# Norm factor of batch 6 taken through DRAM like batch 7's, in a replanned order (linear attention, RMS norm and gated convolution FFN on one core)

## Chip, core and metric

The kernel runs on one core of one Trainium2 chip. The metric is the device time of one execution in microseconds (us). The program is fully unrolled: each engine (PE for matmuls, DVE, ACT, POOL, and SP, which here only issues DMAs) has its own queue of instructions that it works off in order, and semaphores tie the queues together.

## The reference

For each of 8 batches and 8 heads, with 576 rows and head size 64:

```python
kv  = einsum('bhsd,bhse->bhde', k, v)            # 64 x 64 per head
out = einsum('bhsd,bhde->bhse', q, kv)
x   = out / sqrt(mean(out*out, -1) + 1e-6) * g_norm      # per head and row
x   = x.transpose(0, 2, 1, 3).reshape(B, S, 512)
h    = relu(x @ w_in)                                    # 512 -> 1024
conv = sum over 3 rows of conv_w * h (zero padded)       # per channel
y    = (h * sigmoid(conv)) @ w_out                       # 1024 -> 512, float32
```

## The kernel before, in words

Channels lie on partitions, rows on the free axis. Heads go in pairs (four tiles `t` of 128 channels), the 1024 hidden channels in eight tiles `f`, and batches in pairs `p` for the FFN. `ORDER` is a string of tokens that is written out by hand or by a planner; a loop calls one small function per token, in that order, and the order in the string is also the order on every engine's queue. A token reads `name.arguments@slots:choice`: the slots are PSUM banks or the numbers of ring buffers, and the choice says whether ACT or DVE makes a copy or a relu. So a wait of one token holds up all later tokens on the same engine.

The tokens that matter here:

- `Lq`, `Lk`, `Lv` (L301), `Li` and `Lo` load q, k, v of a batch, quarters of `w_in` and halves of `w_out`. POOL issues them. A full batch needs three loads of 576 KB in bf16.
- `kv` (L358) makes the 64 x 64 states on PE. For batches 0 to 3, `qt`/`qc` transpose q on PE, `ot` multiplies. For batches 5, 6 and 7, `dq` (L436) transposes q by two DMAs from SP, `kvn` copies the state out of PSUM, `kx` (L449) copies it with halves swapped by two small DMAs from SP, and `oq` (L464) multiplies in 64 x 64 array tiles.
- `sq` and `oc` (L493, L341, on ACT) square and copy the product out of PSUM.
- The norm factor: `ss` (L575) sums the squares on PE for a group of batches (`NORM`: batch 6 is group 3, batch 7 group 4), `ln` (L584) takes the reciprocal root on ACT. After that there are two ways to spread the factor over the 64 channels of a head. **By PE:** `sl` (L591 to L594) splits it on DVE into bf16 parts, `sp` (L603) multiplies these with a 0/1 matrix, eight products for a batch, and `mu` (L629) multiplies x with the factor in PSUM. **Through DRAM** (batches in `FD`): `fw` (L610) writes the root to DRAM, `fr` (L617) reads it back broadcast to 64 partitions, two DMAs for each half of the rows, and `mu` (L625) multiplies with the factor in SBUF. Both DMAs are issued by SP.
- `hm` (L640) is the first FFN product, eight matmuls for one `f` of one batch, `re` (L646, L648) its relu, `ta`, `aa`, `ab`, `sg`, `mg` the convolution, sigmoid and gate on DVE and ACT (`cm`, L714, makes some of it on PE), `om` and `oh` (L744, L759) the second product, `ea` and `eh` its copy out of PSUM, `st` and `sh` (L778, L773) the stores, issued by SP.
- `unread` (L427) runs matmuls whose result nobody reads.

Of the kernel before, what the change touches and what calls it, by code (L numbers as in the profile page):

```python
# [67 lines left out]
pre@0,0,0 unread.10@0 qt0.0.0@0 ps pn qc0.0.0:1@0 pi ca.k.0 ca.v.0 kv.0.0.1@1 kvc.0.0.1.0:1@0 kvc.0.0.1.1 al.h0@0
ct@2 pg qt0.0.1@3 Lq.1.0@1 qc0.0.1:1 ot.0.0@0 Li.1 pc dg.6:1 sq.0.0@0 Li.3 unread.3@4 kv.0.1.1@3 kvc.0.1.1.0:1
dg.7:1 kvc.0.1.1.1:1 al.h1@1 Lv.1.0@1 al.x0@0 on.0.0@4 nl.0.0@0 mu0.0.0 Lk.1.0@1 Li.0 al.x1@1 unread.1@6 qt0.0.2@2  # L70
ot.0.1@6 sq.0.1@1 Lq.1.2 unread.3@3 kv.0.2.1@3 kvc.0.2.1.0:1 on.0.1@4 qt0.0.3@0 kvc.0.2.1.1:1 qc0.0.2:1@1 nl.0.1@1
mu0.0.1 ot.0.2@2 unread.3@1 kv.0.3.1@1,4 Lv.1.2 sq.0.2@2 qc0.0.3:1 kvc.0.3.1.0:1 kvc.0.3.1.1 on.0.2@6 ot.0.3@4
nl.0.2@2 mu0.0.2 sqh.0.3.0@3 unread.3@0 onh.0.3.0@6 sqh.0.3.1 nlh.0.3.0@3 onh.0.3.1 qt.1.0@2 nlh.0.3.1 qc.1.0:1@2
muh.0.3.0 muh.0.3.1 hm.0.2@6 re.0.2 hm.0.3@4 hm.0.6@6 re.0.3 ta.0.2@0 pl re.0.6 Lk.1.2 ta.0.3 aa.0.1 hm.0.7@4
re.0.7:1 cm.0.6@6 kv.1.0.2@2 kvc.1.0.2.0:1@1 sg.0.6@1 Lq.2.0@0 cm.0.7@4 kvc.1.0.2.1 Lv.2.0@0 ot.1.0@2 sg.0.7
hm.0.1@6 sq.1.0@4 qt.1.1@4 ab.0.1 on.1.0@0 nl.1.0@4 Lk.2.0@0 re.0.1:1 hm.0.0@6 re.0.0 qc.1.1@3 mg.0.3 mu0.1.0
ot.1.1@4 sq.1.1@5 kv.1.2.2@0 ta.0.0@1 kvc.1.2.2.0 kvc.1.2.2.1 on.1.1@2 nl.1.1@5 Li.2 ta.0.1 ot.1.2@0 Lq.3.0@1
ot.1.3@6 Lv.3.0@1 Lk.3.0@1 sq.1.2@6 aa.0.0 sq.1.3@7 mu0.1.1 ab.0.0 unread.1@2 on.1.2@2 nl.1.2@6 on.1.3@4 nl.1.3@7
sg.0.1 sg.0.0 qt.2.1@2 qt.2.0@4 mu0.1.2 mu0.1.3 hm.1.2@0 hm.1.3@6 re.1.2 qc.2.0@4 qc.2.1@0 mg.0.0 ta.1.2@1 hm.1.1@2
hm.1.6@0 re.1.3 kv.2.0.4@6 ta.1.3 aa.1.1 hm.0.5@4 ab.1.1 sg.0.2 re.1.1 sg.0.3 re.1.6 kvc.2.0.4.0@0 sg.1.3  # L80
kvc.2.0.4.1:1 mg.0.1 Lo.0 hm.0.4@0 ot.2.2@6 re.0.5 Lo.1 re.0.4:1 sg.1.2 mg.1.1 ta.0.4@0 ot.2.0@4 sq.2.2@0 sq.2.0@1
ta.0.5 hm.1.7@2 hm.1.4@0 re.1.7 oc.2.2@0 aa.0.2 hm.1.5@2 ot.2.1@6 re.1.4 ta.1.4@1 ab.0.2 oc.2.0@1 Lq.4.0@0 re.1.5
sq.2.1@2 qt.3.1@0 oc.2.1 sg.0.4 sg.0.5 qt.3.0@4 hm.1.0@2 ot.2.3@6 ta.1.5 qc.3.1@1 Lq.5.0@1 unread.3@0 kv.3.0.4@0
qc.3.0@2 aa.1.2 mg.0.2 sq.2.3@3 ss.2@1 kvc.3.0.4.0:1@1 kvc.3.0.4.1:1 oc.2.3 re.1.0 ln.8@0 unread.3@4 ot.3.1@2
ot.3.2@6 ot.3.0@4 ta.1.0@0 ta.1.1 ab.1.2 sq.3.2@4 oc.3.2@2 om.0.0.0@0 om.0.1.0@1 om.0.3.0@6 sq.3.0@5 oc.3.0@3
ot.3.3@4 aa.1.0 sl.8@0 om.0.1.4 sq.3.1@6 ab.1.0 om.0.3.4 oc.3.1 Lk.4.0@0 sq.3.3@7 oc.3.3 sp.2.1@2,4 ea.0.1@0
Lv.4.0@0 ea.0.3@1 mu.2.1.0 dq.5.0@3 ss.3@7 Lv.5.0@1 ln.1@0 om.0.0.4 mu.2.1.1 sp.2.0@6,2 om.0.2.0@1 qtp.4.1@4
mu.2.0.0 sg.1.5 ea.0.0@2 mu.2.0.1 hm.2.7@6 sg.1.4 om.0.2.4 qc.4.1@4 re.2.7 ea.0.2@3 sg.1.0 sg.1.1 sl.1@0 hm.2.2@4
sp.3.0@0,6 mg.1.2 mu.3.0.1 hm.2.5@2 mu.3.0.0 mg.1.0 re.2.2 cm.1.6@6 re.2.5 cm.1.7@0 dq.5.1@0 sg.1.6@1 hm.2.4@2
sg.1.7 sp.3.1@0,6 kv.4.0.4@4 mg.1.3 re.2.4 kvn.4.0.4 qtp.4.0@2 mu.3.1.0 Lk.5.0@1 ky.4.0.4.0 ky.4.0.4.1 mu.3.1.1  # L90
qc.4.0@2 hm.3.4@0 al.x2@0 hm.3.5@6 oq.4.0@2 re.3.4 re.3.5 ta.2.4@0 oq.4.1@0 hm.2.6@4 ta.2.5 sq.4.0@0 oc.4.0@1
hm.3.3@6 hm.3.6@2 re.2.6 sq.4.1@1 re.3.3 Lk.7.0@0 oc.4.1 Lv.7.0@0 hm.3.7@4 hm.3.1@0 re.3.6 aa.2.2 re.3.7 ab.2.2
om.0.6.0@4 hm.3.2@2 sg.2.5 re.3.1 sg.2.4 ta.2.6@1 ta.2.7 Lq.7.0@0 om.0.6.4 oq.4.3@0 oq.4.2@6 kv.5.0.4@5 re.3.2
aa.2.3 ea.0.6@4 Lk.6.0@1 ab.2.3 hm.2.3@2 Lv.6.0@1 sq.4.2@2 om.0.4.0@4 kvn.5.0.4:1 ky.5.0.4.0:1 ky.5.0.4.1:1 sq.4.3@3
oc.4.2@0 oq.5.0@6 oc.4.3 re.2.3 oq.5.1@0 sq.5.0@4 mg.2.2 sq.5.1@5 om.0.8.0@5 om.0.4.4 oc.5.0@3 st.0.0 ss.4@2 oc.5.1
oq.5.3@6 ea.0.4@5 oq.5.2@0 ta.2.2@0 sq.5.3@6 sq.5.2@7 om.0.8.4 ta.2.3 om.0.5.0@4 ss.5 om.0.5.4 ln.2@0 hm.2.0@2
# [5 lines left out]
hm.5.0@0 sg.2.0 sg.2.1 ta.3.2@1 re.5.0 Lq.6.0@1 ta.3.3 hm.5.5@6 hm.4.7@2 aa.3.1 re.4.7 hm.4.0@4 re.4.0 hm.4.1@0
hm.5.6@4 re.5.5 ab.3.1 mg.2.0 re.4.1 dq.7.1@2 st.0.4 kx.6.0.4.0 hm.5.4@6 om.1.5.0@0 ta.3.0@0 sg.3.2 sg.3.3 st.0.6
st.0.3 re.5.4 oq.7.3@2 re.5.6 oq.7.2@6 sq.7.3@2 kx.6.0.4.1 om.1.8.0@1 dq.6.0@4 dq.6.1@3 ta.3.1 st.0.5 sq.7.2@3
st.0.2 st.0.1 ea.1.5@5 oc.7.2@0 ss.7@4 om.1.4.0@0 hm.5.7@6 ln.4@0 oc.7.3 oq.6.0@2 oq.6.2@4 ea.1.4@4 ea.1.8@1 mg.3.1
# [6 lines left out]
re.6.0 st.1.5 st.1.2 hm.6.1@6 re.6.3 re.7.4 re.6.1 st.1.6 aa.4.3 hm.7.1@2 mg.3.3 re.7.1 ab.4.3 sg.4.7 hm.6.4@4
hm.7.5@2 st.1.1 hm.7.0@6 hm.6.5@0 sg.4.6 re.6.4 re.7.0 st.1.3 re.7.5 om.2.4.0@4 re.6.5 om.2.7.0@5 om.2.1.0@0
ta.4.2@0 ta.4.3 om.2.2.0@1 aa.4.1 ea.2.4@5 mg.4.3 ab.4.1 om.2.0.0@4 ta.4.0@1 ta.4.1 sg.4.2 om.2.5.0@2 sg.4.3 aa.4.0
mg.4.1 ab.4.0 ta.4.4@0 ea.2.7@3 ea.2.1@4 ea.2.2@6 ta.4.5 st.2.4 sg.4.1 sg.4.0 st.1.0 st.2.7 st.2.2 aa.4.2 ab.4.2
ea.2.0@0 om.2.3.0@3 ea.2.5@5 om.2.6.0@2 om.2.8.0@4 sg.4.5 mg.4.0 st.0.8 st.2.5 om.3.4.0@5 sg.4.4 mg.4.2 ea.2.6@2
ea.2.3@3 om.3.7.0@3 om.3.4.4 ea.2.8@6 st.2.1 om.3.7.4 om.3.0.0@4 om.3.3.0@2 om.3.0.4 om.3.6.0@1 om.3.5.0@0 om.3.6.4
st.2.6 st.1.8 st.2.8 ea.3.4@7 ea.3.7@5 om.3.5.4 st.2.0 st.3.4 om.3.1.0@3 st.2.3 om.3.3.4 om.3.1.4 om.3.2.0@5
ea.3.0@4 ea.3.6@2 oh.3.8.0@6 ea.3.5@1 ea.3.3@6 om.3.2.4 oh.3.8.1 ea.3.1@0 st.3.5 st.3.7 st.3.6 st.3.0 eh.3.8.0@7
ea.3.2@3 st.3.3 st.3.1 sh.3.8.0 eh.3.8.1 st.3.2 sh.3.8.1  # L120
"""


# [705 lines left out]
```

## Time and profile before

| | |
|---|---|
| median of 3 runs | 179.23 us (179.04 to 180.67) |
| the profiled execution | 179.07 us, span 177.3 us, granted clock 1.0 |
| PE busy | 170.7 us (96% of the span), 1663 matmuls |
| ACT busy | 150.4 us (85%), 233 instructions |
| DVE busy | 138.4 us (78%), 235 instructions |
| POOL busy | 30.6 us (17%), 54 instructions |
| DMA queues | software 59.2%, SP's 27.4% of 16 engines' span |
| `dq`, from issue to landing: shortest, median, longest | 3.7, 10.9, 15.8 us |

The span is the time from the first to the last profiled instruction; 1.8 us of the execution lie around it. A busy PE is not a PE at its peak, since matmuls overlap in the array; what counts for PE is the time from the start of one product to the start of the next. A time such as 36.73 us is counted from the start of the span.

### The profile page before, as it was taken

The page shows a single profiled execution, that of the slowest core. Times are in us where ns is not written, and L with a number is a line of the kernel's source. Part 1 is how long each engine was busy: PE and PEld are TensorE (multiplying, and loading weights), DVE is VectorE, ACT ScalarE, POOL GpSimd, SP SyncE. Part 2 cuts the span into 40 slices and gives each one's busy share as a digit, 9 for nine tenths or more (in the row PEclk, how much of TensorE's full clock was granted, in tenths as well). Part 3 has the DMA queues.
Part 4 walks back from the last instruction along what each step waited for, and adds up shares of the span by engine and source line. Part 5 has one row for each costly group of instructions (what it writes and reads, how often), then busy time and mean ns, then how long its engine had stood idle before and what let it go on. Part 6 is the DMA issues. An engine that isn't in the chain of part 4 may idle for free.

```text
span 177.3 us, 4089 instructions
## 1 busy us (share of the span) xinstructions
PE 170.7 (96%) x1663; PEld 101.8 (57%) x1663; DVE 138.4 (78%) x235; ACT 150.4 (85%) x233; POOL 30.6 (17%) x54
## 2 busy tenths in 40 slices
...
GB/s 144 198 199 199 200 204 204 203 204 206 205 204 203 197 191 141 190 204 204 189 165 123 117 203 132 33 180 292 153 118 0 4 0 178 122 153 307 14 276 199
DMA packets 36219, 29.49 MB, mean 166 GB/s; under 512 B 8528, under 2 KB 31720, under 8 KB 36200
## 3 DMA queue, kind: packets, MB, share of 16 engines
q0 software_dynamic: 21760, 15.96, 59.2%
q1 hardware_dynamic: 14400, 13.26, 27.4%
q8 instruction: 13, 0.21, 0.5%
q14 instruction: 6, 0.05, 0.1%
...
## 4 chain that ended last, share of the span: by engine, by line
PE 76%; DMA 14%; POOL 5%; ACT 2%; issue 1%; POOLq 0%; ACTq 0%
PE bank L744 33%; PE bank L640 30%; DMA w_in_sb<-in_moe_w_in_dram 9%; DMA k_sb<-in_k_dram 5%; PE bank L358 2%; PE bank L464 2%; POOL q_sb L241 1%; PE bank L603 1%; PE bank L575 1%; POOL k_sb L241 1%; POOL v_sb L241 1%; PE bank L759 1%; PE bank L431 1%; PE bank L714 1%; POOL w_in_sb L315 1%
## 5 line engine op out<-in xcount | busy, mean ns | idle before, releaser
L640 PE MATMUL bank<-xT,w_in_sb 128*128 128x288 bf16 x512 | 66.4, 286 | 0.1
L744 PE MATMUL bank<-w_out_sb,h 128*128 128x512 bf16 x280 | 64.5, 379 | 0.0
L640 PEld LDWEIGHTS <-w_in_sb 128*128 128x128 bf16 x512 | 49.1, 98 | 14.7 <-issue 0.6
L744 PEld LDWEIGHTS <-h 128*128 128x128 bf16 x280 | 26.3, 98 | 30.7 <-issue 2.1
L646 ACT ACTIVATE h<-bank 128x576 bf16<-128x576 f32 x61 | 37.9, 657 | 3.1 <-PE bank L640 2.6
L728 ACT ACTIVATE taps<-taps,cwn 128x1152 bf16<-128x1152 bf16 (+1 forms) x36 | 38.0, 1093 | 1.4 <-DVE taps L695 1.3
L341 ACT ACTIVATE row<-bank 128x512 f32<-128x512 f32 (+1 forms) x37 | 21.0, 589 | 11.7 <-PE bank L744 10.0
L734 DVE TENSOR_TENSOR h<-h,taps 128x2304 bf16<-128x2304 bf16 (+1 forms) x20 | 22.3, 1114 | 3.0 <-ACT taps L728 1.8
L689 DVE TENSOR_TENSOR taps<-taps 128x2304 bf16<-128x2304 bf16 (+1 forms) x18 | 20.9, 1160 | 0.4
L695 DVE TENSOR_TENSOR taps<-taps,h 128x2304 bf16<-128x2304 bf16 (+1 forms) x18 | 20.8, 1153 | 0.2
L682 DVE TENSOR_SCALAR taps<-h,cwn 128x1152 bf16<-128x1152 bf16 (+1 forms) x36 | 17.4, 483 | 2.5 <-ACT h L646 2.4
L493 ACT ACTIVATE sq<-bank 128x576 bf16<-128x576 f32 x28 | 17.9, 674 | 0.0
L629 DVE SCALAR_TENSOR_TENSOR xT<-o,cw,bank 128x576 bf16<-128x576 f32 x20 | 15.4, 810 | 2.1 <-PE bank L603 1.9
L683 DVE TENSOR_SCALAR taps<-h,cwn 128x1152 bf16<-128x1152 bf16 (+1 forms) x36 | 16.9, 469 | 0.0
L341 ACT ACTIVATE o<-bank 128x576 f32<-128x576 f32 x24 | 16.0, 682 | 0.0
...
L427 PE MATMUL bank<-fill 128*128 128x512 bf16 x30 | 10.1, 462 | 1.6 <-DVE fill L228 1.5
L301 POOL DMA_DIRECT2D k_sb<-in_k_dram x8 | 6.0, 750 | 26.5 <-PE bank L358 25.7
L301 POOL DMA_DIRECT2D q_sb<-in_q_dram x8 | 6.1, 760 | 17.4 <-PE bank L380 15.1
L358 PEld LDWEIGHTS <-k_sb 96*64 96x64 bf16 x384 | 7.2, 114 | 3.0 <-issue 2.4
L358 PE MATMUL bank<-v_sb,k_sb 96*64 96x64 bf16 x384 | 8.5, 199 | 0.0
L562 DVE SCALAR_TENSOR_TENSOR xT<-bank,cw,root 128x576 bf16<-128x576 f32 x7 | 5.6, 814 | 1.8 <-ACT root L542 1.7
...
## 6 DMA issues: line engine op xcount, KB each, us to landing
...
```

Source lines behind the costliest of these rows:

```text
L341: nc.scalar.activation(to, fr, AX.Copy)
L358: nc.tensor.matmul(ps[i][i * D:(i + 1) * D, t - t0, :], k_sb[:, 2 * t + i, r * D:(r + 1) * D], v_sb[:, 2 * t + i, r * D:(r + 1) * D], star ...
L493: nc.scalar.activation(in_order(b, s), product(b, t), AX.Square)
L640: nc.tensor.matmul(ps[:, e, :HS], w_in_sb[:, t, f * P:(f + 1) * P], x[:, t, e * HS:(e + 1) * HS], start=(t == 0), stop=(t == NT - 1))
L646: nc.scalar.activation(to, fr, AX.Relu)
L682: nc.vector.tensor_scalar_mul(tap[:, 0, f % 2, :n, 8:8 + S], h[:, f], cwn[:, 0, f:f + 1])
L683: nc.vector.tensor_scalar_mul(tap[:, 1, f % 2, :n, :S], h[:, f], cwn[:, 2, f:f + 1])
L689: nc.vector.tensor_add(tap[:, 1, :, :n, :S], tap[:, 0, :, :n, 7:7 + S], tap[:, 1, :, :n, 1:1 + S])
L695: nc.vector.tensor_add(y, y, h[:, 2 * j:2 * j + 2])
L728: nc.scalar.activation(y, y, AX.Sigmoid, scale=cwn[:, 1, f:f + 1])
L734: nc.vector.tensor_mul(h, h, T["tap", c, j][:, 1, :, :n, :S])
L744: nc.tensor.matmul(T["om", p, m], h[:, f, m * P:(m + 1) * P], w_out_sb[:, f, :], start=(f == 0), stop=(f == NF - 1))
```

## The change

`FD` becomes `(6, 7)`. Batch 6's factor now goes the way that batch 7's goes: `fw.3`, and `fr.6.0`, `fr.6.1` (four DMAs) are added to SP's queue, into the rings of the k tiles that are free by then. `sl.3` (four DVE instructions) and `sp.6.0`, `sp.6.1` (eight products) are gone, and batch 6's four `mu` read SBUF instead of PSUM. One of 30 `unread` matmuls is gone. Thirteen copies and relus change between ACT and DVE. Everything else is the same set of tokens in a new order, with new banks. Cut to what is spoken of below:

```diff
-FD = (7,)
+FD = (6, 7)
 ...
 ORDER = """
...
-oc.5.2@2 oc.5.3 ea.0.5@6 re.2.0 dq.7.0@1 hm.2.1@0 aa.2.1 ea.0.8@7 ab.2.1 re.2.1 sl.2@0 sp.4.1@6,2 mu.4.1.1 mu.4.1.0
-om.0.7.0@4 sp.4.0@0,2 kv.7.0.4@5 mu.4.0.0 om.0.7.4 mu.4.0.1 sg.2.3 sp.5.0@0,6 sg.2.2 kvn.7.0.4:1 ea.0.7@2 mu.5.0.1
...
-sq.6.0@4 fw.4 fr.7.0@0 st.1.4 aa.3.0 re.5.7 oc.6.0@3 ta.3.4@1 sq.6.2@5 om.1.6.0@0 oc.6.2@2 oq.6.3@6 oq.6.1@2
-om.1.7.0@1 sq.6.1@6 ta.3.5 ab.3.0 sq.6.3@7 aa.3.2 ab.3.2 ss.6@4 oc.6.3 ln.3@0 sl.3@0 oc.6.1 ea.1.7@6 om.1.0.0@5
-om.1.2.0@1 mu.7.0.1 mu.7.0.0 sg.3.0 sg.3.1 sp.6.0@2,6 mu.6.0.0 mu.6.0.1 fr.7.1@1 mg.3.0 om.1.3.0@4 st.0.7 st.1.7
-ea.1.2@3 hm.4.6@6 ea.1.3@0 om.1.1.0@4 ea.1.6@4 re.4.6 ea.1.0@2 mu.7.1.0 sp.6.1@6,0 mu.7.1.1 ta.3.6@0 mu.6.1.1 sg.3.5
-ta.3.7 al.h3@1 hm.7.3@2 mu.6.1.0 ea.1.1@6 hm.7.7@4 hm.7.6@0 sg.3.4 aa.3.3 hm.6.2@6 re.7.3 re.7.7 hm.6.6@4 re.7.6
...
+om.0.8.4 sq.5.3@7 om.0.6.0@0 oc.5.2@3 ss.5 om.0.6.4 hm.2.0@2 aa.2.1 ln.2@0 ab.2.1 kv.7.0.4@1 ea.0.8:1@5 oc.5.3
...
+st.0.6 mu.5.1.0 mu.5.1.1 kx.7.0.4.0 om.0.5.0@5 sg.2.7 sg.2.2 sg.2.3 sp.4.0@6,0 mu.4.0.0 om.0.5.4 ea.0.5@7 ea.0.4@6
+mu.4.0.1 hm.3.0@2 dq.7.0@2 kx.7.0.4.1 hm.4.4@6 st.0.2 mg.2.1 sp.5.0@4,0 al.h2@0 mu.5.0.0 mu.5.0.1 re.3.0 hm.4.2@2
+hm.4.0@4 st.0.1 dq.7.1@0 ta.2.0@1 sg.2.6 re.4.4 ta.2.1 mg.2.3 re.4.2 oq.7.0@0 oq.7.1@6 re.4.0 kv.6.0.4@2 sq.7.0@0
+hm.5.2@4 oc.7.0@1 sq.7.1@1 oc.7.1 kvn.6.0.4:1 aa.2.0 hm.5.3@0 re.5.2 oq.7.2@2 re.5.3 sq.7.2@2 oq.7.3@6 ta.3.2@0
...
+oc.6.3 ss.6@1 st.0.7 om.1.4.0@4 ab.3.0 ln.3@0 om.1.1.0@1 fw.3 fr.7.1@1 sg.3.5 sg.3.4 re.5.6 ea.1.1@5 fr.6.0@0
+om.1.5.0@5 hm.4.7@2 mu.7.0.1 mu.7.0.0 mg.3.2 om.1.3.0@1 st.1.1 st.1.8 sg.3.1 ta.3.6@1 re.4.7 ea.1.0@6 mu.7.1.1
+st.1.2 ea.1.4@4 ta.3.7 mu.7.1.0 fr.6.1@1 om.1.7.0@0 oc.6.1 sg.3.0 ea.1.3@5 al.h3@1 hm.7.3@6 ea.1.5@2 hm.7.7@2
+ea.1.7@7 re.7.3 aa.3.3 mu.6.0.0 ab.3.3 mu.6.0.1 hm.7.1@0 hm.7.0@6 mg.3.0 re.7.7 sg.3.7 hm.7.2@2 hm.7.6@4 mu.6.1.0
+mu.6.1.1 sg.3.6 re.7.1 hm.6.2@0 re.7.0 re.7.2 re.6.2 hm.6.3@2 hm.7.4@0 hm.6.6@6 re.6.3 hm.6.1@2 re.7.6 re.6.6 re.7.4
...
 """
```

Three orders that the text needs and the cut lines show only in part. Loads before: q of batch 2, v, k, then the last quarter of `w_in` (`Li.2`), then q, v, k of batch 3; after: q of batch 2, `Li.2`, v, k, then v, k, q of batch 3. SP before: ..., `dq.7.0`, `kx`, `kx`, `dq.7.1`, `st.0.4`, ...; after: `st.0.6`, `kx.7.0.4.0`, `dq.7.0`, `kx.7.0.4.1`, `st.0.2`, `st.0.1`, `dq.7.1`. PE before: `oq.7.0`, `kv.6`, `oq.7.1` from 96.43 us on, then nine `hm` and an `om`, then `oq.7.3` and `oq.7.2` at 108.45 us; after: `oq.7.0`, `oq.7.1`, `kv.6`, two `hm`, `oq.7.2`, `oq.7.3`.

More of the change, by code (lines that the diff above doesn't have):

```diff
@@ L62 @@
 QUAD = QD + QP
-FD = (7,)
+FD = (6, 7)
 CONV = {0: (0, 1), 1: (1, 1), 2: (2, 2), 3: (4, 2), 4: (6, 2)}
 ORDER = """
[L68 to L96, printed above, removed]
@@ L97 @@
-oc.5.2@2 oc.5.3 ea.0.5@6 re.2.0 dq.7.0@1 hm.2.1@0 aa.2.1 ea.0.8@7 ab.2.1 re.2.1 sl.2@0 sp.4.1@6,2 mu.4.1.1 mu.4.1.0
-om.0.7.0@4 sp.4.0@0,2 kv.7.0.4@5 mu.4.0.0 om.0.7.4 mu.4.0.1 sg.2.3 sp.5.0@0,6 sg.2.2 kvn.7.0.4:1 ea.0.7@2 mu.5.0.1
-hm.3.0@2 mu.5.0.0 kx.7.0.4.0 re.3.0 al.x3@1 hm.4.4@6 al.h2@0 re.4.4 mg.2.1 sp.5.1@4,0 mu.5.1.0 kx.7.0.4.1 mu.5.1.1
-hm.4.3@2 hm.4.2@6 ta.2.0@0 sg.2.7 hm.5.3@4 sg.2.6 re.4.2 hm.5.2@0 re.5.3 re.4.3 ta.2.1 oq.7.0@6 re.5.2 sq.7.0@0
-oc.7.0@1 kv.6.0.4@4 oq.7.1@0 hm.5.1@2 sq.7.1@1 oc.7.1 mg.2.3 aa.2.0 kvn.6.0.4:1 hm.4.5@6 re.5.1 re.4.5 ab.2.0
@@ L102 @@
[L102 to L105, printed above, removed]
-sq.6.0@4 fw.4 fr.7.0@0 st.1.4 aa.3.0 re.5.7 oc.6.0@3 ta.3.4@1 sq.6.2@5 om.1.6.0@0 oc.6.2@2 oq.6.3@6 oq.6.1@2
@@ L107 @@
-om.1.7.0@1 sq.6.1@6 ta.3.5 ab.3.0 sq.6.3@7 aa.3.2 ab.3.2 ss.6@4 oc.6.3 ln.3@0 sl.3@0 oc.6.1 ea.1.7@6 om.1.0.0@5
-om.1.2.0@1 mu.7.0.1 mu.7.0.0 sg.3.0 sg.3.1 sp.6.0@2,6 mu.6.0.0 mu.6.0.1 fr.7.1@1 mg.3.0 om.1.3.0@4 st.0.7 st.1.7
-ea.1.2@3 hm.4.6@6 ea.1.3@0 om.1.1.0@4 ea.1.6@4 re.4.6 ea.1.0@2 mu.7.1.0 sp.6.1@6,0 mu.7.1.1 ta.3.6@0 mu.6.1.1 sg.3.5
-ta.3.7 al.h3@1 hm.7.3@2 mu.6.1.0 ea.1.1@6 hm.7.7@4 hm.7.6@0 sg.3.4 aa.3.3 hm.6.2@6 re.7.3 re.7.7 hm.6.6@4 re.7.6
-mg.3.2 re.6.2 re.6.6 ab.3.3 hm.6.7@6 re.6.7 hm.7.4@4 hm.7.2@6 hm.6.0@0 sg.3.6 hm.6.3@2 sg.3.7 ta.4.6@1 ta.4.7 re.7.2
@@ L112 @@
[L112 to L120, printed above, removed]
+pre@0,0,0 unread.10@0 qt0.0.0@0 pn ps Lq.1.0@1 pi ca.k.0 ca.v.0 kv.0.0.1@1 qc0.0.0:1@0 ct@2 kvc.0.0.1.0:1@0
@@ new lines @@
+qt0.0.1@3 kvc.0.0.1.1 qc0.0.1:1 pg ot.0.0@0 unread.3@4 kv.0.1.1@3 sq.0.0@0 dg.7:1 pc kvc.0.1.1.0:1 Li.3 on.0.0@4
+al.h0@0 al.x0@0 al.h1@1 unread.1@6 qt0.0.2@2 dg.6:1 kvc.0.1.1.1:1 nl.0.0@0 ot.0.1@6 mu0.0.0 sq.0.1@1 unread.3@3
+kv.0.2.1@3 on.0.1@4 qc0.0.2:1@1 kvc.0.2.1.0 kvc.0.2.1.1:1 nl.0.1@1 qt0.0.3@2 ot.0.2@0 unread.3@3 kv.0.3.1@3,4
+sq.0.2@2 qc0.0.3:1 mu0.0.1 Lk.1.0@1 Lv.1.0@1 kvc.0.3.1.1 on.0.2@6 kvc.0.3.1.0:1 Li.1 ot.0.3@4 nl.0.2@2 mu0.0.2
+sqh.0.3.0@3 sqh.0.3.1 unread.3@2 onh.0.3.0@6 al.x1@1 nlh.0.3.0@3 muh.0.3.0 onh.0.3.1 qt.1.0@0 nlh.0.3.1 qc.1.0:1@2
@@ new lines @@
+muh.0.3.1 hm.0.6@6 re.0.6 hm.0.7@4 cm.0.6@6 kv.1.0.2@0 kvc.1.0.2.0:1@1 kvc.1.0.2.1:1 re.0.7 cm.0.7@4 sg.0.6@0
+ot.1.0@0 hm.0.2@2 sq.1.0@4 Lq.1.2 qt.1.1@6 sg.0.7 re.0.2 on.1.0@4 nl.1.0@4 mg.0.3 Li.0 qc.1.1@3 hm.0.3@2 ta.0.2@1
+mu0.1.0 re.0.3 hm.0.0@6 ta.0.3 Lv.1.2 re.0.0 ot.1.1@4 ta.0.0@0 sq.1.1@5 hm.0.1@2 re.0.1 Lk.1.2 kv.1.2.2@6
+kvc.1.2.2.0 aa.0.1 kvc.1.2.2.1 ta.0.1 on.1.1@0 unread.2@7 ot.1.2@6 nl.1.1@5 aa.0.0 mu0.1.1 ot.1.3@2 sq.1.2@6 ab.0.0
+sq.1.3@7 ab.0.1 unread.1@0 on.1.2@0 on.1.3@4 nl.1.2@6 nl.1.3@7 mu0.1.2 Lq.2.0@0 sg.0.1 sg.0.0 mu0.1.3 qt.2.0@0 Li.2
@@ new lines @@
+qt.2.1@4 hm.1.2@6 qc.2.0@4 qc.2.1@0 Lv.2.0@0 Lk.2.0@0 re.1.2 hm.1.3@2 re.1.3 mg.0.0 hm.0.5@0 hm.1.6@6 ta.1.2@0
+sg.0.2 sg.0.3 ta.1.3 re.1.6 aa.1.1 re.0.5 hm.0.4@2 re.0.4 kv.2.0.4@6 ab.1.1 mg.0.1 kvc.2.0.4.0:1@0 hm.1.0@0 sg.1.3
+sg.1.2 ta.0.4@1 kvc.2.0.4.1 hm.1.7@2 ot.2.2@6 ot.2.0@4 pl re.1.0 ta.0.5 hm.1.1@0 mg.1.1 aa.0.2 Lv.3.0@1 Lk.3.0@1
+re.1.7 hm.1.5@2 sq.2.2@0 ta.1.0@0 ab.0.2 sq.2.0@1 re.1.1 oc.2.0@0 sg.0.4 oc.2.2@1 hm.1.4@0 sg.0.5 kv.3.0.4@4 re.1.5
+Lq.3.0@1 ta.1.1 aa.1.0 re.1.4 ab.1.0 Lo.0 ot.2.3@6 unread.2@5 ot.2.1@2 qt.3.0@0 sq.2.3@2 kvc.3.0.4.0:1@1 mg.0.2
```

27 lines of the change are left out of this document (added).

## The prediction, as put on record before the run

> **What bounds the kernel now.** I read the page's table of engines first, then the chain of waits in order of time, then the waits of each engine, then the timelines of PE, SP and DVE where the change works. Busy time and share of each engine, from the page:
>
> ```profile
> PE 170.7 (96%) x1663; PEld 101.8 (57%) x1663; DVE 138.4 (78%) x235; ACT 150.4 (85%) x233; POOL 30.6 (17%) x54
> ```
>
> The chain that ended last, in order of time (start, length, what):
>
> ```profile
> 20.48 16.20 DMA w_in_sb<-in_moe_w_in_dram
> 36.69 0.05 issue
> 36.73 2.13 PE bank L640 x16
> ...
> 48.44 0.03 ACTq L493
> 48.47 0.06 issue
> 48.53 0.50 ACT rs L584
> ```
>
> Until 36.7 us the chain is a load, from there PE, with one visit to ACT at 48.4 us. So PE's stream sets the end, and the start is paced by loads: `Li.2` lands at 36.69, `hm.0.5` starts at 36.73.
>
> The timelines of SP and PE (start, length, engine, line):
>
> ```profile
> 82.78 1.34 SPq L436 DMA_TRANSPOSE qT<-q_sb  x1
> 90.28 1.18 SPq L449 DMA_DIRECT2D kvx<-kvn  x2
> 91.55 1.33 SPq L436 DMA_TRANSPOSE qT<-q_sb  x1
> ...
> 96.43 0.31 PE L464 MATMUL bank<-qT,kvn 64*64 64x288 bf16 x1
> ```
>
> The same six transposes in the view of their line:
>
> ```profile
> DMA to landing us min/median/max: 3.7/10.9/15.8
> ```
>
> Batch 7's first transpose is issued when its q lands (82.78) and lands at 93.83, in time for `oq.7.0` at 96.43. Under load a transpose takes 11 us, alone 3.7.
>
> The timelines of ACT, DVE and PE around batch 6's factor (in brackets the idle time ahead and what ended it):
>
> ```profile
> 118.78 0.50 ACT L584 ACTIVATE rs<-bank,eps_sb 128x288 f32<-128x288 f32 x1
> ...
> 119.31 0.31 DVE L591 CAST hi<-rs 128x288 bf16<-128x288 f32 x1 [3.08 <-ACT rs L584]
> ...
> 122.18 0.30 PE L603 MATMUL bank<-wparts,spread 32*128 32x288 bf16 x4
> 122.42 1.90 PE L744 MATMUL bank<-w_out_sb,h 128*128 128x512 bf16 x8
> ...
> 127.21 3.97 PE L640 MATMUL bank<-xT,w_in_sb 128*128 128x288 bf16 x31
> ```
>
> Here `ln.3`, `sl.3` (after 3.08 us of idle DVE) and `sp.6.0`: the old way of batch 6's factor. `hm.7.3` starts at 127.21 without a wait.
>
> **PE's stream, counted.** From the start of one product to the start of the next, rows without a wait agree to 0.02 us: `hm` 0.98, `om` 1.73, a half `om` 0.865, `kv` of a full batch 0.88, `ss` 0.36, `sp` 0.23, `oq` 0.15 (0.23 ahead of a full-array product), and 0.09 more on a full-array product when a product in smaller tiles follows. Added up over the order of tokens this gives 164.8 us before and 164.3 after. `sp.6.0` and `sp.6.1` take 0.32 each with the switch (-0.64), one `unread` 0.22 less; +0.3 comes from products in small tiles that stand apart more often. I count these because PE has no cover; `sl.3` (0.33+0.55+0.34+0.44 = 1.66 us of DVE) and the thirteen moved copies count nothing, because between 36.7 and 143 us PE, not DVE, ends the chain. If DVE came to bound, 1.66 would be the gain. `mu` with the factor in SBUF (L625, 813 ns) costs as much as with PSUM (L629, 810 ns).
>
> **The start.** Before, the last of the loads {q, v, k of batch 2, `Li.2`} is `Li.2`; after it is k, with the same bytes ahead of it, so I let it land at 36.7 too. Then `kv.2` starts. PE work left from that mark: 164.8-28.7 = 136.1 before (`hm.0.5`), 164.3-29.3 = 135.0 after (`kv.2`): **-1.1 us**, the stream's 0.55 included. PE must be there by then: five `hm` and a switch, 5.0 us, lie between `hm.1.2` and `kv.2`, so `hm.1.2` must start by 31.7; before it starts at 31.66, after 2.3 us of waits in batch 1's chain from `kv.1.2.2` (26.2) over `sq`, `on`, `nl` and the scaling. That chain is the same after, with two fills more in its shadow. Bounds: +0.5 (chain late by that) and -0.45 (k lands early and PE finds it so).
>
> From 36.73 to the last product's end (174.0), before spends 1.2 us above the count, 0.4 of it at 48.4 to 53.6 where ACT is behind. After has three relus more on ACT in the first 50 us (3 x 0.53): I walked PSUM banks by hand there and found PE's need ahead of ACT's release by 0.1 to 0.4 us at six places. I take **+0.05**, bounds -0.4 and +0.8.
>
> **Batch 7's transposes, new on the path.** `oq.7.0` is due at 36.73 + 56.4 (stream) + 0.8 (losses above the count; 1.1 before) = 93.9 us, 2.5 earlier than before, `oq.7.2` 3.3 later at 97.2. On SP `dq.7.0` is now behind `st.0.6` (waits for `ea.0.6`) and `kx.7.0.4.0`, which waits for `kvn.7` on DVE, this for `kv.7` (PE done at 85.1) and for `sl.2` ahead of it (ends 85.4). With 0.4 for `kvn` and 0.6 for `kx`: issue at 86.5, against 82.78 before. q itself is in SBUF by 82.7. Bounds of its duration: 3.7 (lands 90.2, no wait) and 11.05 (lands 97.5, 3.6 us of wait). What slowed it before were batch 6's loads, 2.9 us each from 82.7 on, which last to some 91.5 when the transpose is not among them; the trace's DMA packets show two transposes alone moving in 3.5 us (102.5 to 105.95). So 91.5 + 1.75 + 1 us to the landing = 94.2, 0.3 late. `kx.7.0.4.1`, issued behind it, can be as late; `dq.7.1` has two stores of 0.7 us ahead of it and lands by about 97. I take **+0.4**, bounds 0 and 3.6. Behind a late `oq.7.0` stands all of PE.
>
> The Trainium skill, DMA: Bandwidth & Descriptors, section "Queues, rings and completion order", says that each DMA engine takes turns between queues packet by packet, that SP's transfers share one ring per engine in order, and that a completion lands only after that engine's earlier writes. This case's packets agree with the turns: 372 packets of loads and 372 of transposes in each 2 us from 88 us. It speaks against the new order; what it would give is the first rival.
>
> **Batch 6's factor.** After, `ss.6` ends at PE's count 107.8, and `hm.7.3` and `hm.6.2` start at 117.45 and 123.3 of the same count; the offset cancels, so I use counts. `ln.3` 108.0 to 108.5, `fw.3` issued 108.6; landing 1.77 later (112.95 to 114.72 for `fw.4`). `fr.7.1` now stands behind `fw.3`: 109.0, landing 5.4 later (117.01 to 122.37) at 114.4. DVE: `mg.3.2` waits for `ln.3`, a table load (1.29), `sg.3.5` and `sg.3.4` (2 x 1.15) until 112.2, then `mg.3.2` 1.27, `ta.3.6` 0.86, `mu.7.1.1` 0.73, `ta.3.7` 0.86, `mu.7.1.0` 0.8: 116.75, 0.7 ahead of `hm.7.3`. On with `aa.3.3`, `ab.3.3`, `mg.3.0` (1.27 each) and four `mu`: 123.5 for the last, which `hm.6.2` needs 0.6 after its start, at 123.9. `fr.6.0` goes once `fw.3` has landed (110.5) and lands near 116; `fr.6.1` behind three stores, issued 114.6, lands near 120 to 121; needed at 118 and 121.9. Slack 0.4 to 0.9: **+0.1**, bounds 0 and 2.
>
> **The end.** `st.3.3` and `st.3.7` now stand between the last copies and `sh.3.8.1`, where one store stood. Each takes SP 0.4 us, mostly while PE works. **+0.15**, bounds -0.1 and +0.5.
>
> **Sum**, against the profiled execution (span 177.3 and 1.8 around it, 179.07): 179.07 - 1.1 + 0.05 + 0.4 + 0.1 + 0.15 = **178.7 us**, 0.3% under the median of 179.23 (the profiled one lies 0.16 under it). A measurement of this kernel tells about 1%, 1.8 us, from no change.
>
> **Rivals.**
> 1. *Transposes late, slower.* `dq.7.0` keeps its 11.05 us because queues are still shared. For it: the median of 10.9, SP's new order. Against: two of three loads are through when it starts. 97.5 instead of 94.2: 178.7 + 3.3 = **182.0**. It turns the sign from a landing after 94.8. By the skill's turns it holds as long as batch 6's q is still loading at 93 us.
> 2. *Faster by more than 1%.* None of the new waits, the 0.4 at 48.4 us gone, k early: 179.07 - 1.1 - 0.4 - 0.45 = **177.1**. For it: POOL issues these loads 10 us ahead of landing. Against: the same bytes, and small slacks everywhere.
> 3. *Batch 6's factor late.* `fr.7.1` and `fr.6.0` go out together, and the four DMAs of before needed 7.5 us from first issue to last landing (114.86 to 122.37). `fr.7.1` at 7.5: `mu.7.1.1` starts 1.9 late, less 0.7 of slack, and again 0.3 at `hm.6.2`: **180.2**.
>
> **Chances.** Forecast 0.48 (own range 177.6 to 179.9), rival one 0.21, two 0.21, three 0.10. Faster by over 1% (under 177.4): rival two and a little of the forecast's edge, 0.23; slower (over 181.0): most of rival one and an edge of three, 0.22; within 1%: 0.55. The range reaches from rival two to rival one, 177.0 to 181.9.
>
> **What would show it.** After: `kv.2` starts within 0.3 us of 36.7; `dq.7.0` issued near 86.5 and PE's wait ahead of L464 near 94 us under 1 us (over 2: rival one); no wait over 0.5 us of PE for DVE's L625 near 126 and 132 us (else three); DVE's 3.08 us of idle time now in front of L625; eight products of L603 and four L591 to L594 fewer. A PE idle for loads before 36 us, or for ACT between 37 and 55, would break the sum.

## The result, and the profile after

The changed kernel takes 181.87 us (median of 6, 181.13 to 182.95) against 179.27 for the kernel before in the same session: ratio 1.0135, 95% interval 1.0086 to 1.0185. Forecast was 178.7, a little faster; the sign was wrong. (Ratios compare undisturbed executions only, so they need not be the quotient of two medians.) The profiled execution took 181.29 us with a span of 179.5, 2.2 us more than before.

The page after: the engine table, then the costliest group.

```profile
PE 170.4 (95%) x1654; PEld 101.5 (57%) x1654; DVE 137.1 (76%) x230; ACT 150.4 (84%) x234; POOL 30.3 (17%) x54
...
L640 PE MATMUL bank<-xT,w_in_sb 128*128 128x288 bf16 x512 | 67.5, 286 | 2.2 <-ACT row L341 1.7
```

PE and DVE do less, as they should, and the span still grew by 2.2 us. The last line says where: PE stood 2.2 us ahead of `hm`, and 1.7 of that ended when ACT had copied a row out of PSUM (`ea`, L341). That wait didn't exist before.

The chain that ended last, in order of time, at the two places where it leaves PE:

```profile
35.01 1.33 ACT taps L728 x2
...
46.96 0.77 DVE qT L343
...
47.77 0.19 PE bank L430
...
127.53 1.97 PE bank L640 x16
...
129.51 0.57 ACT row L341
```

From 18.7 to 47.8 us the chain now runs almost wholly over ACT and DVE; before, it was a load until 36.7 and PE from there. From 47.8 us it is PE, up to 129.5, where ACT's copy comes in.

Timelines of PE, ACT, DVE and SP around the second place (start, length, engine, line; idle time ahead in brackets):

```profile
127.36 2.12 PE L640 MATMUL bank<-xT,w_in_sb 128*128 128x288 bf16 x16
131.14 5.06 PE L640 MATMUL bank<-xT,w_in_sb 128*128 128x288 bf16 x40 [1.65 <-ACT row L341]
...
117.87 0.50 ACT L584 ACTIVATE rs<-bank,eps_sb 128x288 f32<-128x288 f32 x1 [0.17 <-ACT o L341]
...
129.51 1.57 ACT L341 ACTIVATE row<-bank 128x512 f32<-128x512 f32 x3 [2.06 <-PE bank L640]
...
119.77 1.55 DVE L625 SCALAR_TENSOR_TENSOR xT<-o,cw,factor 128x576 bf16<-128x576 f32 x2 [1.99 <-DMA factor<-factor]
...
118.40 0.33 SPq L610 DMA_DIRECT2D factor<-rs  x1
118.90 2.81 SPq L617 DMA_DIRECT2D factor<-factor  x4
123.13 1.34 SPq L778 DMA_DIRECT2D out_dram<-row  x3
124.58 1.29 SPq L617 DMA_DIRECT2D factor<-factor  x2
```

ACT's 2.06 us of idle time are put down to PE, but those products were long done. What came free just then is a buffer. `ea` copies an output row into one of eight row buffers (the number after its `@`), and `st` stores it; the buffer can be written again when the store has landed. `ea.1.3@5` takes the buffer of `ea.1.1@5`. In the trace `st.1.1` is issued at 123.13, behind `fw.3`, `fr.7.1` and `fr.6.0`, and lands at 129.41; `ea.1.3` starts at 129.51. Next are `ea.1.5@2` (`st.1.8`, landed 129.59) and `ea.1.7@7` (`st.1.2`, 130.04). `ea.1.7` frees PSUM bank 0, which `hm.7.1@0` needs: PE starts it at 131.14, 1.82 us later than its count.

How long those stores took, in the view of their line from 120 to 135 us: first the kernel before, then after.

```profile
L778 SPq DMA_DIRECT2D out_dram<-row x6: 332/335/433, 120.3 to 128.5; - x6
DMA to landing us min/median/max: 2.3/3.8/4.7
```

```profile
L778 SPq DMA_DIRECT2D out_dram<-row x9: 332/431/1111, 123.1 to 131.0; - x9
DMA to landing us min/median/max: 4.4/6.1/6.7
```

And each engine's busy time in stretches, before and then after (columns: stretch, length, PE, PE's weight loads, DVE, ACT, POOL, granted clock, DMA share, GB/s; the share counts the whole time of each packet that starts in the stretch, over 16 DMA engines, so it can pass 1):

```profile
31.00:43.00 12.00, 11.87 (x174) 9.26 (x175) 10.84 (x23) 11.99 (x20) 0.79 (x1) 1.00 1.33 203
43.00:50.00 7.00, 7.00 (x119) 4.00 (x113) 6.95 (x15) 6.97 (x13) 3.85 (x5) 1.00 1.27 207
...
126.00:130.00 4.00, 4.00 (x32) 2.64 (x31) 4.00 (x9) 4.00 (x7) 0.00 (x0) 1.00 0.46 170
```

```profile
31.00:43.00 12.00, 11.75 (x159) 9.05 (x154) 11.56 (x25) 11.92 (x21) 1.11 (x2) 1.00 1.31 204
43.00:50.00 7.00, 6.55 (x128) 3.87 (x127) 6.80 (x13) 6.95 (x14) 2.44 (x4) 1.00 1.26 206
...
126.00:130.00 4.00, 3.49 (x24) 2.15 (x22) 4.00 (x5) 1.94 (x3) 0.00 (x0) 1.00 1.02 312
```

In the last stretch the DMA share went from 0.46 to 1.02 and ACT's busy time from 4.00 to 1.94: the reads of the factor and the stores share the queue, and ACT stands.

**The balance.** Take PE's start of each product, less the counted stream up to it. Where that grows, PE waited. After against before this difference is -0.26 us at 37 us, +0.21 at 54, +0.76 at 95, +0.75 at 130 and +2.58 at the end. With the stream (-0.55) and the end (+0.22: 3.31 us from the last product's end to the span's, 3.09 before) that makes 2.25 us, the difference of the spans.

### The profile page after: what moved, and what is told of

Read it like the earlier page. It is cut to its first block, busy times and chain, and to the rows that moved or that the text cites. A ratio compares the mean times of both kernels' runs of the same rounds, so it can differ in the third digit from the quotient of the medians.

```text
span 179.5 us, 4063 instructions
## 1 busy us (share of the span) xinstructions
PE 170.4 (95%) x1654; PEld 101.5 (57%) x1654; DVE 137.1 (76%) x230; ACT 150.4 (84%) x234; POOL 30.3 (17%) x54
## 4 chain that ended last, share of the span: by engine, by line
PE 68%; ACT 14%; DVE 7%; DMA 6%; issue 3%; ACTq 0%; POOLq 0%
PE bank L744 30%; PE bank L640 26%; ACT h L646 4%; DMA out_dram<-row 3%; DMA q_sb<-in_q_dram 3%; ACT L213 3%; ACT sq L493 2%; PE bank L358 2%; ACT taps L728 2%; PE bank L464 1%; DVE taps L689 1%; ACT row L341 1%; PE bank L431 1%; PE bank L427 1%; PE bank L380 1%
## 5 line engine op out<-in xcount | busy, mean ns | idle before, releaser
L640 PE MATMUL bank<-xT,w_in_sb 128*128 128x288 bf16 x512 | 67.5, 286 | 2.2 <-ACT row L341 1.7
L646 ACT ACTIVATE h<-bank 128x576 bf16<-128x576 f32 x62 | 38.9, 664 | 2.5 <-PE bank L640 2.3
L341 ACT ACTIVATE row<-bank 128x512 f32<-128x512 f32 (+1 forms) x36 | 20.3, 588 | 12.9 <-PE bank L744 9.0
L341 ACT ACTIVATE o<-bank 128x576 f32<-128x576 f32 x23 | 15.6, 682 | 0.0
L629 DVE SCALAR_TENSOR_TENSOR xT<-o,cw,bank 128x576 bf16<-128x576 f32 x16 | 12.1, 809 | 2.0 <-PE bank L603 1.9
L301 POOL DMA_DIRECT2D v_sb<-in_v_dram x8 | 6.0, 750 | 19.5 <-PE bank L358 18.4
L625 DVE SCALAR_TENSOR_TENSOR xT<-o,cw,factor 128x576 bf16<-128x576 f32 x8 | 6.3, 812 | 2.2 <-DMA factor<-factor 2.2
```

Of the source, the lines that this page charges most:

```text
L341: nc.scalar.activation(to, fr, AX.Copy)
L640: nc.tensor.matmul(ps[:, e, :HS], w_in_sb[:, t, f * P:(f + 1) * P], x[:, t, e * HS:(e + 1) * HS], start=(t == 0), stop=(t == NT - 1))
L646: nc.scalar.activation(to, fr, AX.Relu)
```

## Experiments: where the time went

Theories. **A:** a late store holds a row buffer, ACT's copy waits for it, PE for the copy. **B:** the loss lies elsewhere in the new order, and the wait for the buffer only takes up slack. **C:** batch 6's factor itself is late. **D:** ACT is behind because of the three relus it was given (`re.0.7`, `re.0.1`, `re.0.4`).

### The changed kernel again, and three edits of it

`c0_after` is the changed kernel unchanged. `e1_stores`:

```diff
-st.0.8 st.0.4 ... ss.6@1 st.0.7 ... fw.3 ... st.1.1 st.1.8 ... st.1.2 ... ea.1.3@5 ... st.0.3
+st.0.8 st.0.4 st.0.3 ... ss.6@1 st.0.7 st.1.8 st.1.2 ... fw.3 ... st.1.1 ... ea.1.3@3   (3 and 5 swapped from here)
```

`e3_no_fr6` leaves out `fr.6.0` and `fr.6.1`; batch 6 is multiplied with batch 7's factor. `e2_old_fd` is the other way round, the order of before with `FD = (6, 7)`:

```diff
-... sl.3@0 ... sp.6.0@2,6 mu.6.0.0 mu.6.0.1 fr.7.1@1 ... sp.6.1@6,0 ... ta.3.6@0 mu.6.1.1 ... mu.6.1.0
+... fr.7.1@1 fw.3 fr.6.0@0 fr.6.1@1 ... ta.3.6@0 mu.6.0.0 mu.6.1.0 mu.6.0.1 mu.6.1.1
```

> The changed kernel itself once more, beside the next three on the same chip: 1.010 to 1.018 of the kernel before, with PE's wait of 1.6 to 1.9 us ahead of hm.7.1 near 131 us again.

Measured: 182.18 us, 1.0136 (1.0104 to 1.0169), with 1.75 us ahead of `hm.7.1`. The loss repeats at its place.

> The changed kernel with three stores issued earlier (st.0.3 after st.0.4, st.1.8 and st.1.2 ahead of fw.3) and row slots 3 and 5 swapped from ea.1.3 on, so that ea.1.3, ea.1.5 and ea.1.7 find their slots free; the DMAs are the same. Theory A (a late store holds a row slot, so ACT and then PE wait): the wait ahead of hm.7.1 goes, 1.8 us less than the changed kernel, about 1.003 of the kernel before. Rival B (the loss is the new order's in other places, and this wait only takes up slack): under 0.5 us less, 1.010 or more.

Measured: 180.93 us, 1.0100 (1.0062 to 1.0138). By the ratio alone this is B's number, not A's 1.003. The trace says more: the wait ahead of `hm.7.1` is gone, as A has it, and one of 0.89 us, half as long, has come ahead of `hm.6.2`. Timelines of PE, ACT and DVE (its lines are one lower than above):

```profile
134.28 1.98 PE L639 MATMUL bank<-xT,w_in_sb 128*128 128x288 bf16 x14 [0.73 <-ACT h L645]
...
131.29 2.40 ACT L727 ACTIVATE taps<-taps,cwn 128x1152 bf16<-128x1152 bf16 x2 [0.98 <-DVE taps L694]
...
125.14 0.82 DVE L624 SCALAR_TENSOR_TENSOR xT<-o,cw,factor 128x576 bf16<-128x576 f32 x1 [0.67 <-DMA factor<-factor]
...
129.17 0.82 DVE L624 SCALAR_TENSOR_TENSOR xT<-o,cw,factor 128x576 bf16<-128x576 f32 x1 [0.35 <-ACT row L340]
129.90 1.35 DVE L694 TENSOR_TENSOR taps<-taps,h 128x2304 bf16<-128x2304 bf16 x1
```

The chain, in order of time: two more stores stand ahead of `fw.3`, `fr.7.1` and `fr.6.0`. DVE waits 0.67 us at 125.14 for `fr.7.1`, the second half of batch 7's factor (landed 125.05; the same wait was 0.25 us in the changed kernel), and 0.35 us at 129.17, ahead of `mu.6.0.0`, for `fr.6.0` (landed 129.05 instead of 127.07; the view names ACT). `ab.3.3` stands behind both on DVE, ACT's sigmoid waits 0.98 us for that, the relu behind it frees PE's bank. So theory C holds only in part: a late factor is the second wait, by way of DVE and ACT, but more of it is batch 7's second half than batch 6's factor.

> The changed kernel without batch 6's four reads of its factor: batch 6 is multiplied by batch 7's factor, which leaves out only these DMAs (fw.3 stays). Theory A: st.1.1 lands within 3.5 us of its issue instead of 6.3, the wait ahead of hm.7.1 goes, 1.8 us less than the changed kernel, about 1.003. Rival B: same as the changed kernel within 0.5 us. Rival C (batch 6's factor itself arrives late for mu): 0 to 0.5 us less, the wait ahead of hm.7.1 stays.

Measured: 180.47 us, 1.0069 (1.0044 to 1.0094). The nine stores from 120 us on land in 4.4 us (median; 6.1 with the four DMAs), ACT still stands 0.31 us for one, and `hm.7.1` is 0.32 us late instead of 1.82. By the ratios, 1.0136 and 1.0069, half of the loss goes with the four DMAs.

> The kernel before in its own order with batch 6's factor through DRAM alone: sl.3, sp.6.0 and sp.6.1 taken out, fw.3, fr.6.0 and fr.6.1 behind fr.7.1, batch 6's four mu behind ta.3.6. Theory A (the transfers cost only where a row slot is reused early): PE's stream 0.6 us shorter, a wait of 0 to 0.7 us at hm.6.2, 0.996 to 1.002. Rival C (the way through DRAM is late by itself): a wait of over 1 us ahead of hm.7.3 or hm.6.2, 1.006 or more.

Measured: 189.47 us, 1.0553 (1.0524 to 1.0582), far outside both expectations. Timelines of SP and ACT:

```profile
120.25 0.33 SPq L609 DMA_DIRECT2D factor<-rs  x1
125.10 2.58 SPq L616 DMA_DIRECT2D factor<-factor  x4
127.72 10.31 SPq L777 DMA_DIRECT2D out_dram<-row  x7
...
134.97 0.60 ACT L340 ACTIVATE row<-bank 128x512 f32<-128x512 f32 x1 [8.01 <-DMA out_dram<-row]
```

`fr.6.0` has to wait for `fw.3` to land, at the head of SP's queue, from 120.6 to 125.1; the next seven stores stand behind it, and ACT waits 8.01 us for one; PE stands 8.4 us ahead of `hm.7.7` for the copy behind it. It is theory A in large. Batch 6's factor is late here too: DVE waits 3.59 us for `fr.6.0` (landed 132.17) and 1.55 us for `fr.6.1` (134.54), so the run does not say what the loss would be by the stores alone. `fw.4` landed 1.76 us after its issue here, `fw.3`, behind the 2 x 288 KB of `fr.7.1`, 4.8 us after; the changed order sends `fw.3` ahead of `fr.7.1`. The Trainium skill, DMA: Bandwidth & Descriptors, section "Queues, rings and completion order", has SP's queue as one ring on each DMA engine, where descriptors are consumed in ring order; these two landings agree with it.

### Stores earlier, relus back

`e5_rows` moves three stores ahead of `fw.3` and the other DMAs of batch 6's factor and gives eleven copies other row buffers; `e6_relu` puts the three relus back on DVE; `e7_rows_relu` does both; `e8_rows_relu_fr` also moves `st.1.1` and `st.1.2` behind `fr.6.1`.

```diff
 e5_rows
-st.0.3, st.0.0 (late); st.0.7 ... fw.3 ... st.1.8;      ea.0.4@6 ea.1.3@5 ea.1.5@2 ea.1.7@7 ...
+st.0.0 ... st.0.4 st.0.3; st.1.8 st.0.7 ... fw.3;       ea.0.4@1 ea.1.3@1 ea.1.5@3 ea.1.7@2 ...
 e6_relu
-re.0.7 re.0.1 re.0.4
+re.0.7:1 re.0.1:1 re.0.4:1
```

> The changed kernel with row slots that are free when a copy needs them: st.0.0 issued behind dq.5.1, st.0.3 behind st.0.4, st.1.8 ahead of st.0.7, and other slots for ea.0.4, ea.1.3, ea.1.5, ea.1.7 and those that follow. Factor transfers unchanged. Theory A: no wait of ACT on a store at 92 us (0.5 us in the changed kernel) nor at 129 us (2.1 us), PE gains 0.3 to 0.8 at 92 and 1.75 at hm.7.1, of which up to 0.9 comes back at hm.6.2, where fr.6.1 is late: 1.3 to 2 us less than the changed kernel, 1.003 to 1.006 of the kernel before. Rival B: under 0.6 us less, 1.010 or more.

Measured: 179.97 us, 1.0037 (1.0023 to 1.0050), as A has it: PE's waits at `hm.7.1` and at 93 us are gone; 0.28 us stay at `hm.7.7` and 0.48 at `hm.6.2`. No `mu` of batch 6 waits for its factor there (`fr.6.0` landed at 127.81, `mu.6.0.0` starts at 128.88, right behind `aa.3.3`); DVE is late by 0.96 us that it waited for `fr.7.1` (landed 125.19).

> The changed kernel with the three relus re.0.7, re.0.1 and re.0.4 back on DVE, nothing else. Rival D (part of the loss is ACT behind between 42 and 50 us): PE's waits at hm.1.4, ot.2.1, qt.3.0 and ot.3.0, 1.0 us together in the changed kernel, fall to 0.4 or less, but the wait at hm.7.1 stays: 0.3 to 0.6 us less than the changed kernel, 1.010. Theory A alone: no difference, 1.0136.

Measured: 183.66 us, 1.0260 (1.0219 to 1.0302): worse by 1.2% than the changed kernel and outside both expectations, so D's direction is wrong. A timeline line of PE:

```profile
21.77 0.90 PE L713 MATMUL bank<-h,dgw 128*128 128x288 bf16 x6 [1.54 <-DVE h L647]
```

On DVE `re.0.7` stands behind two copies of `kv.1.0`'s states and comes 2.3 us later than it did on ACT (20.96 instead of 18.69); PE needs it in `cm.0.7`.

> Both edits, the row slots and the three relus. If the two losses add: 1.8 to 2.4 us less than the changed kernel, 1.000 to 1.003 of the kernel before, with 0.9 us left at hm.6.2. If only one of them is on the path: no better than the better of the two.

Measured: 1.0203 (1.0165 to 1.0242): on top of e5 the relus cost 1.7%, no less than on top of the changed kernel; the two gains that were to add up (1.000 to 1.003) did not come.

> As the one before, with st.1.1 and st.1.2 behind fr.6.1, so that batch 6's second half of factors goes out right behind the first. If hm.6.2 waits for fr.6.1: the wait there falls by 0.5 us or more, 0.996 to 1.001 of the kernel before. If it waits for DVE's own work: unchanged within 0.2 us.

Measured: 1.0188 (1.0169 to 1.0206): the two stores' place doesn't matter once their buffers are free.

### More row buffers, no transfer moved

This takes the wait away without touching the DMAs.

```diff
 f1_slots
-ea.0.4@6  ea.1.3@5 ea.1.5@2 ea.1.7@7
+ea.0.4@11 ea.1.3@8 ea.1.5@9 ea.1.7@10
 f2_slots_nofr6: f1_slots without fr.6.0 and fr.6.1
 f3_slots_late:  f1_slots with  fr.6.1 st.1.1 st.1.8 st.1.2
```

> The changed kernel with four more row buffers, used by four of ACT's copies (ea.0.4, ea.1.3, ea.1.5, ea.1.7); no DMA and no token is moved. Theory A (a store that lands late holds a row buffer, ACT's copy waits for it, and PE for the bank): PE's 1.8 us ahead of hm.7.1 and the 0.2 to 0.5 us ahead of sp.5.0 go, although the stores land as late as before; up to 0.9 us comes back at hm.6.2, which needs the second half of batch 6's factor (landed 131.9 us): ratio 1.003 to 1.008. Theory B (the waits only take up slack of the new order): 1.011 or more. Theory C (batch 6's factor itself is late): hm.7.1's wait goes, and all of it comes back at hm.6.2: 1.011 or more, with the wait there above 1.5 us.

Measured: 179.26 us, 0.9980 (0.9954 to 1.0007), better than A's range. PE, and the stores' line from 120 to 135 us:

```profile
127.14 9.07 PE L639 MATMUL bank<-xT,w_in_sb 128*128 128x288 bf16 x72
```

```profile
L777 SPq DMA_DIRECT2D out_dram<-row x9: 332/432/1243, 122.9 to 130.4; - x9
DMA to landing us min/median/max: 5.3/6.2/6.7
```

The stores land as late as before (median 6.2 us), and PE runs nine `hm` without a wait. The span is 177.5 us, 2.0 less; the ratios differ by 1.6% or 2.8 us, as the profiled execution of the changed kernel (181.29) was one of its quicker ones. Nothing came back at `hm.6.2`: DVE waits 0.15 us for `fr.7.1`, not at all for `fr.6.0` (landed 127.07) and 0.18 us for `fr.6.1` (132.03). B and the direct form of C are out.

> As the last, and without the four DMAs that read batch 6's factor back (batch 6 is multiplied with batch 7's factor instead). A: neither a row buffer nor a factor is waited for from 110 us on; what is left over the kernel before is the new order's own loss at 42 to 50 and 88 to 94 us (0.3 to 0.8 us) less PE's shorter stream (0.55 us) plus the end (0.15 us): ratio 0.999 to 1.003. B: as without the four DMAs alone, 1.006 or more.

Measured: 0.9978 (0.9953 to 1.0003), the same as with the four DMAs, and a little under its expected range. They cost nothing that these runs can tell once no buffer waits behind them.

> As the first of these (four more row buffers), with three stores (st.1.1, st.1.8, st.1.2) moved behind the second half of batch 6's factor on SP's queue, so that fr.6.1 is issued some 3 us earlier. A with C as its second wait: fr.6.1 lands before 129 us, hm.6.2 waits under 0.2 us, nothing waits for the late stores: 0.999 to 1.004. If the factor's landing is set by the transfers and not by its place in the queue, it lands at 131 us as before and the wait at hm.6.2 stays at 0.5 to 0.9 us: 1.005 to 1.008. B: 1.011 or more.

Measured: 0.9979 (0.9951 to 1.0008). `fr.6.1`, issued 1.35 us behind `fr.6.0` (3.99 in f1), took 8.7 us to land instead of 7.7, `fr.6.0` 7.1 instead of 6.7. Of the 2.6 us of earlier issue, 1.6 are left at the landing, and the ratio doesn't change. PE waits 0.31 us at `hm.6.2`, where DVE had waited 0.51 us for `fr.7.1`. The expected landing before 129 us did not come.

> The changed order with batch 6's factor spread by PE again: sl.3 behind ln.3, sp.6.0 and sp.6.1 with their mu ahead of hm.7.7 and hm.7.0, and no fw.3, fr.6.0, fr.6.1. A and C (the loss comes from the five added DMAs, directly or through the stores behind them): the stores land in under 4 us, hm.7.1 waits under 0.4 us, PE's stream is 0.55 us longer again: 1.002 to 1.009. B (the loss is the new order's): 1.012 or more.

```diff
-fw.3 ... fr.6.0@0 ... fr.6.1@1 ... hm.7.7@2 ... mu.6.0.0 ... hm.7.1@0 hm.7.0@6 ... mu.6.1.0
+sl.3@0 ... sp.6.0@2,4 mu.6.0.0 mu.6.0.1 hm.7.7@2 ... hm.7.1@0 sp.6.1@4,6 mu.6.1.0 mu.6.1.1 hm.7.0@6
```

Measured: 1.0252 (1.0178 to 1.0327). The time is inconclusive: up to 128 us PE goes as in the changed kernel; then the banks that I gave `sp.6.0` and `sp.6.1` cost 1.0 and 2.6 us of PE's waits for `mu`. It tells what my placing costs, not what the order does. Two of A's signs can be read from the trace all the same: with eight row buffers and without the five added DMAs the stores from 120 us on land in 3.7 us (median), and no copy waits for one.

### Controls

> The kernel before with twelve row buffers instead of eight, each copy (ea, eh) given the buffer whose store is earliest in SP's order. Theory A: no copy of the kernel before waits for a store in its trace, so more buffers bring nothing: 0.997 to 1.003. Rival E (more buffers help any order, so that the gain with them says nothing on the change): 0.996 or less.

Measured: 1.0011 (0.9995 to 1.0027): the kernel before gains nothing from twelve row buffers (`ea` and `eh` spread over `@0` to `@11`).

> The changed kernel with twelve row buffers for all of its copies in the same way. A: as with four more for the four copies, 0.995 to 1.001, no wait of a copy for a store. B: 1.004 or more.

Measured: 0.9990 (0.9970 to 1.0010). No copy waits for a store. (In this trace 0.40 us are left at `hm.6.2`, behind 0.61 us of DVE's wait for `fr.7.1`.) Against the kernel before, this version and f1 can't be told from no change.

> The changed kernel with one more row buffer, for ea.1.3 alone, so that only the copy that waited 2.06 us for st.1.1 is freed. A: the next copies (ea.1.5 behind st.1.8, landed 129.6 us, and ea.1.7 behind st.1.2, landed 130.0 us) then wait in its place; without its own wait ACT would come to ea.1.5 at 128 us, so ACT still waits some 1.6 us there, 2.0 us at the most: ratio 1.008 to 1.013. If one buffer was the whole cause: 1.000 to 1.004, the rest being ea.0.4.

```diff
-ea.1.3@5
+ea.1.3@8
```

Measured: 181.97 us, 1.0150 (1.0122 to 1.0178). ACT's timeline:

```profile
128.08 0.63 ACT L340 ACTIVATE row<-bank 128x512 f32<-128x512 f32 x1
130.47 1.08 ACT L340 ACTIVATE row<-bank 128x512 f32<-128x512 f32 x2 [1.76 <-DMA out_dram<-row]
```

`ea.1.3` goes on time, and `ea.1.5` then waits 1.76 us for `st.1.8`: the wait moves to the next buffer of the same burst. (The ratio is a little above the expected range; in this execution `ea.0.4` also waited 1.19 us, 0.48 in the changed kernel.)

### The smaller loss at 42 to 48 us

All three on `g2_after_ring12`, with one or two relus as `re.0.4:1`, `re.0.1:1`.

> The changed kernel with twelve row buffers (0.999 by itself), and re.0.4 back on DVE as in the kernel before. In the changed kernel the chain goes over ACT from 31 to 42.5 us and over DVE from there to 47.7. If ACT's load alone makes PE late there, 0.53 us less of it gives up to 0.5 us: 0.995 to 0.998. If both engines are full (ACT 6.95 and DVE 6.80 of 7 us from 43 to 50), DVE's 0.7 us more comes out behind it: 0.999 to 1.003.

> The same with re.0.1 back on DVE instead (26.8 us on ACT). ACT's load alone: 0.995 to 0.998. Both full: 0.999 to 1.004.

> The same with both of them on DVE. ACT's load alone: 0.993 to 0.997. Both full: 1.000 to 1.006; then what is left of the loss of the kernel with three relus on DVE (1.012 times the changed kernel's) comes from re.0.7, for which PE waited 1.5 us.

Measured: 1.0048 (1.0021 to 1.0075), 1.0037 (1.0006 to 1.0068) and 1.0082 (1.0055 to 1.0109). The first and the last lie above both of their expected ranges. Beside g2's 0.9990, each relu less on ACT costs time. In h1 PE's waits at 42 to 48 us stay (1.05 us) and 0.6 us more come at `ot.2.2`, at 40.5. ACT's extra relus are not what makes PE late there; DVE is as full, as its 11.56 of 12 us from 31 to 43 (in the changed kernel and in g2) say.

## Why the prediction was wrong, point by point

- **PE's stream** (164.3 instead of 164.8): right; the changed kernel's products show the counted steps. The path over DRAM does take that time off PE.
- **The start** (-0.55 beyond the stream): half right. `kv.2` started at 37.03 (36.7 was predicted), and the difference at that mark is -0.26. What I took for the pacing load isn't: the chain before 47.8 us goes over ACT and DVE.
- **36.7 to 55 us** (+0.05, bounds -0.4 and +0.8): mis-sized, +0.47. The step that failed in this term is the sentence that DVE's part counts nothing since PE ends the chain. That was read from the old chain. In the new order DVE is busy 11.56 of 12 us from 31 to 43 us (10.84 before), and from 42.6 to 47.7 us it is DVE that ends last. I had walked ACT's releases there, not DVE's. No run takes work off DVE at this place, so that the loss is DVE's rests on the chain alone.
- **Batch 7's transposes** (+0.4; rival one, 182.0): did not happen. `dq.7.0` was issued at 87.63; its landing isn't in the trace, but `kx.7.0.4.1`, issued behind it, landed at 93.60, and `oq.7.0` started at 95.44 without a wait. The median time to landing in the view of L436 fell from 10.9 to 7.8 us. (The equal packet counts that I gave for "each 2 us from 88 us" hold for 88 to 90; from 90 to 92 the loads have 285 and SP's queue 558.) That the time came out near 182.0 is chance: rival one's place shows no wait. What PE lost near there, 0.5 us at 88 to 94, was the same kind of row-buffer wait: `st.0.6` landed at 92.12 and `ea.0.4@6` started at 92.20; with a buffer of its own (f1) the waits at `sp.5.0` and `hm.4.2` are gone.
- **Batch 6's factor** (+0.1, bounds 0 and 2; rival three, 180.2): this is the step that failed and that decided the time. I wrote that `fr.6.1` stands "behind three stores" and followed the queue only until the factor lands. I never asked the other way round: which stores stand behind `fw.3`, `fr.7.1` and `fr.6.0`, when *they* land, and who waits for their buffers. That chain (DMA, store, row buffer, ACT, PSUM bank, PE) cost 1.82 us at `hm.7.1` and has no term in the sum and no rival; I had put it at nothing without a reason. Four more buffers remove it (1.0135 to 0.998) with the transfers unchanged; one buffer doesn't. DVE's idle time ahead of L625 (1.99 us at 119.77, for `fr.7.0`) came as foreseen. Batch 6's factor itself comes in time: `fr.6.0` landed at 127.07 for a `mu` at 128.18, `fr.6.1` at 131.87 for one at 132.18. What rival three feared for `fr.7.1` exists in small: DVE waits 0.25 us for it at 124.59, and where that wait is 0.5 to 1.0 us (f3, g2, e1, e5), PE stands 0.3 to 0.9 us at `hm.6.2`.
- **The end** (+0.15): right, +0.22.
- **The sum.** The places that I had terms for, as measured, give -0.55 - 0.26 + 0.47 + 0.55 + 0.22 = +0.4 against the forecast -0.4, and the missing term adds 1.8. But the 0.55 at 88 to 94 us is a row-buffer wait too: the two together are 2.4, and without them the sum is -0.1. They make the sign. Without buffer waits the time is 0.998 and 0.999 of before's, where the forecast was 0.998; both intervals hold 1, so whether the change gains a little or nothing stays open. By the balance, what it takes off PE (-0.55 and -0.26) comes back nearly whole between 37 and 54 us and at the end (+0.47 and +0.22).
